# One activation tile and the keys' weight loaded from ScalarE's queue in a linear-attention and MLP kernel on one core

## The chip, the cores and the metric

The kernel runs on 1 core of one Trainium2 chip. The metric is the device time of one execution in microseconds (us), the median over runs. The engines are called as the profile calls them: PE (matmuls), PEld (PE's weight loads), DVE, ACT, POOL, and SP, which here only issues DMAs; "SPq" and "ACTq" mark DMAs issued from SP's and from ACT's instruction stream.

## The reference

```python
def reference(A_x, A_wqkv, A_wo, B_x, B_w1, B_w2):     # x: 1 x 2048 x 512, bf16
    qkv = layernorm(x) @ wqkv                          # 512 -> 3 * 512, 32 heads of 16
    pq, pk = phi(q), phi(k)    # phi(t) = where(t > 0, t + 1, exp(t)) + 1e-6
    kv = einsum("bhsd,bhse->bhde", pk, v)
    z = einsum("bhsd->bhd", pk)
    o = einsum("bhqd,bhde->bhqe", pq, kv) / (einsum("bhqd,bhd->bhq", pq, z) + 1e-6)
    h = x + o @ wo
    return h + maximum(layernorm(h) @ w1, 0) @ w2      # 512 -> 1792 -> 512
```

B_x is not used. Layernorm has no scale and no shift.

## The kernel before

The 2048 rows of x are 16 tiles of 128 rows by 512 columns (128 KB each), tile t lying in `x_nat[:, t, :]`. Four tiles make a chunk, whose transposed layernorm is `lnT[c]`.

Nothing is scheduled by a program at build time: `ORDER`, a string of some 700 words, is read from left to right, and each word calls one small function, which records its instructions on their engines. So the order of words is the order of instructions on every engine, and a word that must wait holds up all later words of the same engine. The digits behind a word's name are its arguments: tile, number of tiles, PSUM bank.

```python
    def op_lx(t, n):
        nc.sync.dma_start(out=x_nat[:, t : t + n, :], in_=rows_of(xf, t, n))
    def op_ax(t, n):
        nc.scalar.dma_start(out=x_nat[:, t : t + n, :], in_=rows_of(xf, t, n))
    def op_ak(k, n):
        nc.scalar.dma_start(out=wk_sb[:, k : k + n, :], in_=wqkv_v[:, k : k + n, D : 2 * D])
    op_lk = lambda k, n: load_d(wk_sb, wqkv_v[:, :, D : 2 * D], k, n)
    ...
    for word in ORDER.split():
        name, *idx = word.split(".")
        ops[name](*map(int, idx))
```

The words at the program's head, with the line that the profile shows for each:

- `lx` (L219) loads tiles of x from SP's queue, `ax` (L222) from ACT's. `lk` (L225, the line of the helper `load_d`) loads the keys' weight, 512 x 512, 512 KB, from SP's queue, `ak` (L228) from ACT's. `lq`, `lv`, `lo`, `l1`, `l2` (all L225) load the other weights from SP's queue.
- `table` (L183) loads ACT's function tables. `const` (L191 to L195) fills constants on DVE, `masks` (L199 to L211) fills masks on POOL. `warm` (L250) runs matmuls on zeros, whose results nobody reads.
- `S.t` (L253) and `A.t` (L254), on DVE: mean and variance of tile t. `R.t` (L259, L260), on ACT: the reciprocal deviation, two instructions. `N.t` (L267), on DVE: the normalised tile.
- `T.t` (L292), on PE: four 128 x 128 transposes of tile t into a bank. `E.t` (L302), on ACT: that bank into `lnT`. From tile 5 on `X.t` (L313) does the same by a transposing DMA from SP's queue.
- `K.t` (L321), on PE: the keys of tile t, four matmuls of 128 x 512 against `wk_sb`. `F`, `U` (L339, L342, ACT), `M`, `D` (L346, L349, DVE) make phi of them. `Q` (L329) are the queries, `G` (L373) the matmuls that gather the keys' statistics.

After them come attention's small products, the MLP's two matmuls (L516 and L525, then L545) and the stores. `T.0`, `T.1`, `T.2` stand ahead of `K.0` on PE, then `K.0`, `K.1`, `T.3` and `K.2`.

A DMA issued from SP or ACT waits where its completion counter is still in use by an earlier DMA; there are eight such counters, handed out in turn.

Of the kernel before, what the change touches and what calls it, by code (L numbers as in the profile page):

```python
# [15 lines left out]


ORDER = """
table const lx.0.1 warm.66.7.64 lx.1.1 masks lx.2.1 lk.0.4 lx.3.1 S.0 lx.4.2 S.1 lx.6.2 lq.0.4 A.0 A.1 S.2 R.0.1
warm.2.7 lx.8.4 R.1.1 N.0 lx.12.4 A.2 N.1 T.0.1 R.2.1 T.1.6 E.0 N.2 E.1 T.2.4 S.3 K.0.2 E.2 A.3 S.4 K.1.4.2.2 R.3.1  # L20
K.1.4.0.2 F.0.1 N.3 A.4 U.0.1 S.5 T.3.5 K.2.6.2.2 E.3 S.7 K.2.6.0.2 F.1.1 K.3.3.0.2 M.0.1 A.5 U.1.1 D.0.1 K.3.3.2.2
M.1.1 R.4.2 Q.0.3.1 S.6 F.3.1 A.7 A.6 N.5 F.2.1 Q.0.1.5 N.4 X.5 R.6.2 D.1.1 T.4.7 U.3.1 M.2.1 Q.0.0.4 M.3.1 S.8 E.4
lo.0.2 U.2.1 S.10 Q.0.2.0 qF.0.0.2 N.6 K.4.2 N.7 X.6 A.10 A.8 qU.0.0.2 S.9 K.5.3 D.3.1 X.7 A.9 D.2.1 R.8.2 G.0 S.15
F.4.2 N.8 G.1 S.13 X.8 U.4.2 S.14 G.3 qU.0.2.2 A.13 S.12 lv.0.2 G.2 M.4.2 A.12 N.9 K.7.3 R.12.2 A.15 D.4.2 X.9
qF.0.2.2 K.6.2 N.12 A.14 S.11 R.14.2 X.12 K.8.0 F.6.2 N.15 N.14 G.4 A.11 N.13 U.6.2 M.6.2 X.13 qM.0.0.2 K.9.1 R.10.2
qD.0.0.2 K.12.2 X.15 D.6.2 U.8.2 za.4.1 G.5 F.8.2 X.14 K.13.3 N.11 N.10 za.6.0 G.6 X.11 U.12.2 G.7 M.8.2 F.12.2 X.10
qM.0.2.2 K.14.0 D.8.2 M.12.2 K.15.1 lv.2.2 za.8.0 l1.0.2 K.11.3 l1.2.2 F.14.2 D.12.2 K.10.2 zf U.14.2 qD.0.2.2 G.9 zhi
F.10.2 M.14.2 G.13 zlo U.10.2 G.8 M.10.2 D.14.2 G.12 D.10.2 z.0.0 z.2.0 z.3.0 z.1.0 G.15 zc zh d4.0.2 G.11 dl4.0 dx4.0
G.14 wb.0 G.10 lo.2.2 Q.1.1.1 gA.2.2 gD.0.2 rb.0.4 Q.1.0.0 ab.0.1 rb.0.6 ab.0.3 kv.1.7 rb.0.2 kv.3.7 ab.0.7 kv.0.7
rb.0.0 kv.2.7 ab.0.5 Q.1.3.3 l2.7.7 kx qF.1.0.2 Q.1.2.2 qU.1.0.2 qM.1.0.2 m.0.4 m.2.6 m.1.5 qF.1.2.2 qD.1.0.2 m.3.7  # L30
Q.2.0.0 mD.0.2 mA.2.2 Q.2.1.1 qU.1.2.2 dm.0.0.2 Q.2.3.7 dm.0.2.2 qF.2.0.2 h.1.6 qM.1.2.2 qD.1.2.2 qU.2.0.2 h.0.2 hD.1
d4.1.4 s.1 Q.3.1.5 a.1 hD.0 nA.1 h.3.0 s.0 dl4.1 x.1 h.2.2 a.0 hD.3 nA.0 Q.2.2.6 s.3 dx4.1 x.0 Q.3.2.0 a.3 hD.2
qF.2.2.2 n.3 wb.1 Q.3.3.1 s.2 qU.2.2.2 x.3 Q.3.0.4 a.2 n.2 qF.3.2.2 qM.2.0.2 x.2 qM.2.2.2 ph.0.3.3.0 qU.3.2.2 qD.2.2.2
ph.0.0.6.0 ph.0.1.7.0 qM.3.2.2 rb.1.7 qU.3.0.2 ph.0.2.2.0 qD.3.2.2 rb.1.3 ph.0.11.1.0 rb.1.5 qD.2.0.2 ph.0.10.0.0
qF.3.0.2 rb.1.6 ph.0.10.0.1 rb.1.1 ph.0.11.1.1 rb.1.0 p.0.5.4 pD.0.10.2 rb.1.4 rb.1.2 ph.0.2.2.1 ph.0.3.3.1 l2.0.7
qM.3.0.2 ph.0.0.6.1 pD.0.2.2 p.0.6.0 ph.0.1.7.1 qD.3.0.2 p.0.4.3 pD.0.0.2 p.0.7.1 pA.0.4.2 dm.1.2.2 d4.2.5.2 dm.1.0.2
p.0.8.2 dl4.2 pD.0.6.2 dl4.3 p.0.9.3 dx4.2 p.0.13.5 dx4.3 pD.0.8.2 wb.2 r.0.4 h.4.7 h.6.0 hD.4 rb.2.3 f.3.1.0.7 rb.2.1
s.4 rb.2.0 a.4 rb.2.6 rb.2.2 p.0.12.4 rb.2.5 rb.2.7 h.7.2 pD.0.12.2 rb.2.4 f.3.1.7.7 wb.3 hD.7 s.7 h.5.4 hD.6
f.2.3.7.7 hD.5 f.1.6.0.7 dm.2.2.2 dm.2.0.2 s.6 rb.3.2 h.8.0 rb.3.7 a.6 s.5 f.1.6.7.7 rb.3.0 hD.8 rb.3.5 rb.3.6 n.4 s.8
rb.3.3 f.2.3.0.7 a.5 rb.3.1 fo.1 rb.3.4 n.5 a.7 x.5 h.9.7 n.7 n.6 fo.2 f.0.0.7.7 x.4 fo.3 dm.3.2.2 h.10.5 x.7 dm.3.0.2  # L40
h.11.6 hD.9 x.6 hD.10 h.13.3 s.10 h.15.2 fd.3.0.2 fd.3.2.2 a.10 a.8 n.10 hD.11 h.14.7 x.10 s.11 f.0.0.0.7 n.8 a.11
hD.15 s.9 p.1.3.5 hD.13 p.1.8.2 hD.14 fo.0 p.1.2.4 s.15 h.12.1 s.14 p.1.9.3 s.13 a.13 p.1.7.7 pD.1.8.2 p.1.6.6 a.9
n.11 r.8.4 n.13 p.1.12.0 n.9 r.4.4 a.14 a.15 x.9 n.14 p.1.11.3 hD.12 pD.1.2.2 p.1.13.1 x.11 p.1.10.2 n.15 pD.1.6.2 x.8
p.1.0.5 pD.1.10.2 p.1.5.4 fd.1.0.2 fd.1.2.2 x.14 p.1.1.6 s.12 pD.1.12.2 f.5.2.7.7 fd.2.0.2 fd.2.2.2 fd.0.0.2 fd.0.2.2
x.15 pD.1.0.2 p.1.4.3 p.2.2.5 pD.1.4.2 f.5.2.0.7 p.2.6.3 fo.5 p.2.7.4 p.2.3.6 pD.2.6.2 p.2.10.1 a.12 n.12 r.12.4
p.2.4.4 pD.2.2.2 x.12 f.7.0.0.7 fd.5.0.2 fd.5.2.2 x.13 f.7.0.7.7 p.2.5.5 fo.7 p.2.11.2 pD.2.4.2 p.2.12.3 pD.2.10.2
p.2.13.4 f.4.6.0.7 pD.2.12.2 p.2.0.5 p.3.2.1 p.3.3.2 f.4.6.7.7 f.6.0.0.7 fo.4 pD.3.2.2 p.3.9.7 p.3.8.6 f.6.0.7.7
pD.3.8.2 p.2.9.1 fo.6 p.2.1.6 fd.6 p.3.1.3 p.3.0.2 p.2.8.0 pD.3.0.2 p.3.11.4 pD.2.0.2 p.3.10.3 pD.2.8.2 p.3.5.2
p.3.6.6 pD.3.10.2 p.3.7.7 p.3.4.1 pD.3.6.2 f.8.3.0.7 pD.3.4.2 p.3.13.7 f.10.5.0.7 p.3.12.6 f.10.5.7.7 pD.3.12.2
f.14.4.0.7 fo.10 fd.10 fd.7 f.15.1.0.14.3.1 f.15.6.0.14.0.2 fo.15.3.1 fd.15.3.1 f.14.4.7.7 fd.4 f.8.3.7.7 f.13.0.0.7  # L50
f.9.7.0.7 f.13.0.7.7 f.11.5.7.7 fo.13 fo.15.0.2 fo.14 fd.15.0.2 f.11.5.0.7 fd.13 fo.8 fd.8 f.9.7.7.7 fo.11 f.12.1.0.7
fo.9 fd.9 fd.11 f.12.1.7.7 fd.14 f.15.2.0.14.2.1 fo.12 fd.12 fo.15.2.1 ad.15.2.1
"""


# [543 lines left out]
```

## Time and profile before

| | before |
|---|---|
| device time, median of 3 runs (lowest to highest) | 168.88 us (168.74 to 168.93) |
| profiled execution: its time | 168.48 us |
| profiled execution: its span | 166.8 us |
| PE busy | 162.6 us, 98% of the span |
| DVE busy | 115.9 us, 69% |
| ACT busy | 49.5 us, 30% |
| 16 DMA engines, queue of SP (q1) | 33.9% of their time |
| 16 DMA engines, queue of ACT (q10) | 0.7% |

The span is what the trace shows, from the first instruction to the last; the profiled execution's own time has 1.7 us more that lies around it. A view of the timeline has start, length, engine, line, operation, output and inputs, shape and count of merged instructions, and in brackets the idle time before them and what ended it. A view by windows has busy time by engine, then the granted PE clock, the share of the DMA engines that was busy, and the rate that they moved. In the chain of waits each row is one piece of the path that ended last. `st` is the output of `S`, `mv` of `A`, `rstd` of `R`, `h_nat` of `N`, `bk` the PSUM banks, `in_A_wqkv_dram` the tensor that holds the weights of queries, keys and values.

### The profile page before, as it was taken

What the parts mean: (1) busy time and instruction counts of PE and PEld (TensorE: products, weight loads), DVE (VectorE), ACT (ScalarE), POOL (GpSimd) and SP (SyncE); (2) the same over time, 40 slices, a digit from 0 to 9 for tenths busy, and PEclk for the clock granted to TensorE, in tenths of its full rate; (3) what the DMA queues carried; (4) which work ended last, traced back from release to release, by engine and by line L of the source; (5) the groups of instructions that cost most, each with busy time, mean ns of one, the idle gap of its engine ahead of it and who ended that gap; (6) DMA issues with size and microseconds to landing.
All of it is one profiled execution on the core that took longest, in us unless ns stands there. A gap on an engine that the chain in (4) does not pass through costs nothing.

```text
span 166.8 us, 2421 instructions
## 1 busy us (share of the span) xinstructions
PE 162.6 (98%) x920; PEld 79.8 (48%) x920; DVE 115.9 (69%) x215; ACT 49.5 (30%) x83; POOL 4.8 (3%) x21
## 2 busy tenths in 40 slices
PE   7999999999999999999999999999999999999993
PEld 7544444454544774444444444444444444464442
DVE  3899999942599979668999899564535484400532
ACT  3899996715777916200000020010000000000000
POOL 7400000000000000000000000000000000000000
PEclk9999999999999999999999999999999999999999
DMA  4975555763752446231352035312000000020122
GB/s 113 346 300 126 125 97 103 276 253 96 170 177 51 111 135 210 72 94 56 111 109 69 0 63 93 100 30 64 0 0 4 31 0 0 7 97 2 44 95 73
DMA packets 26811, 16.28 MB, mean 98 GB/s; under 512 B 16176, under 2 KB 25776, under 8 KB 26800
## 3 DMA queue, kind: packets, MB, share of 16 engines
q1 hardware_dynamic: 26336, 15.84, 33.9%
q10 hardware_dynamic: 464, 0.30, 0.7%
q8 instruction: 7, 0.11, 0.3%
q14 instruction: 4, 0.03, 0.1%
HBM read 9.96 MB, written 2.62 MB: 75 GB/s over the span
## 4 chain that ended last, share of the span: by engine, by line
PE 94%; DVE 2%; DMA 1%; ACT 0%; issue 0%
PE bk L545 29%; PE bk L516 26%; PE bk L321 8%; PE bk L373 8%; PE bk L329 8%; PE bk L501 8%; PE bk L525 3%; DMA x_nat<-in_A_x_dram 1%; DVE st L253 1%; PE bk L445 1%; DVE gT L553 1%; PE bk L397 1%; PE bk L292 1%; PE bk L419 1%; PE bk L431 1%; DVE h_nat L267 0%
## 5 line engine op out<-in xcount | busy, mean ns | idle before, releaser
L545 PE MATMUL bk<-w_sb,at 128*128 128x512 bf16 (+2 forms) x252 | 50.9, 355 | 0.0
L516 PE MATMUL bk<-lnT,w_sb 128*128 128x512 bf16 x200 | 45.6, 379 | 0.0
L536 DVE TENSOR_SCALAR at<-bk 128x1024 bf16<-128x1024 f32 x27 | 32.4, 1220 | 13.6 <-PE bk L516 10.6
L545 PEld LDWEIGHTS <-at 128*128 128x128 bf16 x252 | 23.5, 98 | 25.2 <-DVE at L536 0.3
L516 PEld LDWEIGHTS <-w_sb 128*128 128x128 bf16 x200 | 19.5, 98 | 23.1 <-issue 0.4
L553 DVE SCALAR_TENSOR_TENSOR gT<-bk,rstd,h_nat 128x512 bf16<-128x512 f32 (+2 forms) x18 | 12.1, 688 | 22.6 <-PE bk L545 20.2
L339 ACT ACTIVATE eb<-bk 128x1024 bf16<-128x1024 f32 (+1 forms) x18 | 16.6, 930 | 3.5 <-PE bk L419 1.6
L259 ACT ACTIVATE rstd<-mv,eps 128x2 f32<-128x2 f32 (+2 forms) x14 | 4.1, 294 | 44.4 <-DVE mv L256 41.6
L342 ACT ACTIVATE rb<-bk 128x1024 bf16<-128x1024 f32 (+1 forms) x18 | 16.6, 936 | 0.9 <-PE bk L321 0.9
L501 PE MATMUL bk<-m_sb,pqs 128*128 128x512 bf16 x64 | 15.3, 379 | 0.0
L321 PE MATMUL bk<-wk_sb,lnT 128*128 128x512 bf16 x64 | 15.1, 379 | 0.0
L329 PE MATMUL bk<-lnT,wq_sb 128*128 128x512 bf16 x64 | 15.0, 379 | 0.0
L373 PE MATMUL bk<-at,h_nat 128*128 128x512 bf16 x56 | 13.2, 379 | 0.0
L253 DVE BATCH_NORM_STATS2 st<-x_nat 128x6 f32<-128x512 bf16 x16 | 10.5, 675 | 1.9 <-DMA x_nat<-in_A_x_dram 1.9
L507 DVE TENSOR_TENSOR h_nat<-bk,x_nat 128x512 bf16<-128x512 f32 x16 | 10.7, 679 | 0.9 <-PE bk L501 0.8
L255 DVE BATCH_NORM_STATS2 st<-h_nat 128x6 f32<-128x512 bf16 x16 | 10.8, 687 | 0.2
L501 PEld LDWEIGHTS <-pqs 128*128 128x128 bf16 x64 | 6.3, 98 | 7.6
L373 PEld LDWEIGHTS <-h_nat 128*128 128x128 bf16 x64 | 6.1, 98 | 7.3 <-issue 0.2
L321 PEld LDWEIGHTS <-lnT 128*128 128x128 bf16 x64 | 6.0, 97 | 7.4 <-ACT lnT L302 0.3
L329 PEld LDWEIGHTS <-wq_sb 128*128 128x128 bf16 x64 | 6.1, 98 | 7.1 <-issue 0.2
L346 DVE TENSOR_SCALAR eb<-eb 128x1024 bf16<-128x1024 bf16 (+1 forms) x18 | 6.7, 389 | 0.3 <-ACT eb L339 0.3
L267 DVE TENSOR_SCALAR h_nat<-x_nat,mv,rstd 128x512 bf16<-128x512 bf16 x16 | 6.1, 400 | 0.3 <-ACT rstd L260 0.3
(62 smaller groups left out, 90.8 us busy)
## 6 DMA issues: line engine op xcount, KB each, us to landing
w_sb<-in_B_w_dram SPq DMA_DIRECT2D x4, 896.0 KB, 5.0
rr<-scr SPq DMA_DIRECT2D x28, 64.0 KB, 2.6
out_dram<-gT SPq DMA_DIRECT2D x10, 128.0 KB, 1.9
x_nat<-in_A_x_dram SPq DMA_DIRECT2D x2, 512.0 KB, 7.1
out_dram<-gT SPq DMA_DIRECT2D x11, 64.0 KB, 1.6
x_nat<-in_A_x_dram SPq DMA_DIRECT2D x4, 128.0 KB, 2.2
wk_sb<-in_A_wqkv_dram SPq DMA_DIRECT2D x1, 512.0 KB, 4.2
x_nat<-in_A_x_dram SPq DMA_DIRECT2D x2, 256.0 KB, 4.5
```

Of the source, the lines that this page charges most:

```text
L253: op_S = lambda t: nc.vector.bn_stats(out=st[:, t, :], in_=x_nat[:, t, :])
L255: op_s = lambda t: nc.vector.bn_stats(out=st2[:, t, :], in_=h_nat[:, t, :])
L321: nc.tensor.matmul(bk[:, b, :], lhsT=lnT[c][:, kd, j * P : (j + 1) * P], rhs=wk_sb[:, kd, :], **part(("k", t), KD),)
L329: nc.tensor.matmul(bk[:, b, :], lhsT=wq_sb[:, kd, j * P : (j + 1) * P], rhs=lnT[c][:, kd, :], start=(kd == 0), stop=(kd == KD - 1),)
L339: nc.scalar.activation(out=buf(eb, kind, i, n), in_=bank(at_bank[kind, i], n), func=ACT.Exp)
L342: nc.scalar.activation(out=buf(rb, kind, i, n), in_=bank(at_bank[kind, i], n), func=ACT.Relu)
L373: nc.tensor.matmul(bk[:, KD + kd, :], lhsT=ln_nat[:, t, kd * P : (kd + 1) * P], rhs=pk(t)[:, 0, :], start=(not stated), stop=(len(stated) ...
L501: nc.tensor.matmul(bk[:, b, :], lhsT=pqs[:, (c * KD + jb) % NQ, j * P : (j + 1) * P], rhs=m_sb[:, jb, :], start=(jb == 0), stop=(jb == KD ...
L516: nc.tensor.matmul(bk[:, b, :], lhsT=w1_sb[:, kd, f * P : (f + 1) * P], rhs=lnT[c][:, kd, :], start=(kd == 0), stop=(kd == KD - 1),)
L536: nc.vector.tensor_scalar(out=acts[c % 2][:, f : f + n, :], in0=bank(at_bank["p", c, f], n), scalar1=-1.0, scalar2=0.0, op0=ALU.mult, op1= ...
L545: nc.tensor.matmul(bk[:, b, 0 : w * P], lhsT=acts[c % 2][:, f, j * P : (j + 1) * P], rhs=w2_sb[:, f, k * P : (k + w) * P], **part(("f", t, ...
L553: nc.vector.scalar_tensor_tensor(out=o_t[:, t % NO, cols], in0=bk[:, at_bank["f", t, k], 0 : w * P], scalar=rstd2[:, t : t + 1], in1=h_nat ...
```

## The change

Tile 1 of x (`ax.1.1`) and the keys' weight (`ak.0.4`) are issued from ACT's queue, ahead of the load of ACT's tables. Tiles 0, 2, 3 and the rest of x are issued from SP's queue as before, without tile 1 and the keys' weight between them. The whole table of words is then laid out anew around this; no function and no size changes (some PSUM banks do), and each engine has the instructions that it had, save the two DMAs.

```diff
 ORDER = """
-table const lx.0.1 warm.66.7.64 lx.1.1 masks lx.2.1 lk.0.4 lx.3.1 S.0 lx.4.2 S.1 lx.6.2 lq.0.4 A.0 A.1 S.2 R.0.1
+ax.1.1 const lx.0.1 warm.66.7.64 ak.0.4 lx.2.1 masks table lx.3.1 lx.4.2 lx.6.2 S.0 lq.0.4 lx.8.4 S.1 lx.12.4 A.0 A.1
...
```

On ACT, at the program's head, the two DMAs now stand between the first branch (the barrier that starts all engines) and the table load:

```order
 L594 UNCONDITIONAL_BRANCH
+L222 DMA x_nat<-in_A_x_dram 128x512
+L228 DMA wk_sb<-in_A_wqkv_dram 128x4x512
 L183 ACT_TABLE_LOAD
 L259 ACTIVATE rstd<-mv,eps_77 128x1
```

The table load has moved behind two DMA issues, and R.0, the first user of the tables, still follows it.

On SP, at the program's head, the same two loads are gone (x_nat are tiles of x, wk_sb, wq_sb, wo_sb the weights; the row that stands for three single tiles holds tiles 0, 1, 2 before and tiles 0, 2, 3 now):

```order
 L594 UNCONDITIONAL_BRANCH
 L219 DMA x_nat<-in_A_x_dram 128x512 x3
-L225 DMA wk_sb<-in_A_wqkv_dram 128x4x512
-L219 DMA x_nat<-in_A_x_dram 128x512
 L219 DMA x_nat<-in_A_x_dram 128x1024 x2
 L225 DMA wq_sb<-in_A_wqkv_dram 128x4x512
 L219 DMA x_nat<-in_A_x_dram 128x2048 x2
-L313 DMA_TRANSPOSE lnT_86<-h_nat 128x4x128
 L225 DMA wo_sb<-in_A_wo_dram 128x2x512
-L313 DMA_TRANSPOSE lnT_86<-h_nat 128x4x128 x2
+L313 DMA_TRANSPOSE lnT_86<-h_nat 128x4x128 x3
```

Everything behind tile 2 has moved up by one or two places, and the first half of wo now stands ahead of the first transposing DMA instead of behind it.

On DVE the first fifteen instructions after the constants' five are the same in both kernels, from S.0 to S.5. The first difference lies just behind them, where S.5 and S.7 stood together and now phi's first step M.0 (L346) stands between them (the piece starts with N.3 and A.4):

```order
 L267 TENSOR_SCALAR h_nat<-x_nat,mv,rstd 128x512
 L254 BN_AGGR mv<-st 128x2
-L253 BN_STATS st<-x_nat 128x6 x2
-L346 TENSOR_SCALAR eb<-eb 128x512
-L254 BN_AGGR mv<-st 128x2
-L349 TENSOR_TENSOR pk_lo<-rb,eb 128x512
+L253 BN_STATS st<-x_nat 128x6
 L346 TENSOR_SCALAR eb<-eb 128x512
 L253 BN_STATS st<-x_nat 128x6
+L254 BN_AGGR mv<-st 128x2
```

Up to N.4 and N.5 DVE has the same instructions, in another order.

More of the change, by code (lines that the diff above doesn't have):

```diff
@@ L18 @@
 ORDER = """
-table const lx.0.1 warm.66.7.64 lx.1.1 masks lx.2.1 lk.0.4 lx.3.1 S.0 lx.4.2 S.1 lx.6.2 lq.0.4 A.0 A.1 S.2 R.0.1
[L20 to L52, printed above, removed]
+ax.1.1 const lx.0.1 warm.66.7.64 ak.0.4 lx.2.1 masks table lx.3.1 lx.4.2 lx.6.2 S.0 lq.0.4 lx.8.4 S.1 lx.12.4 A.0 A.1
@@ new lines @@
+warm.2.7 S.2 R.0.1 lo.0.2 R.1.1 N.0 A.2 N.1 T.0.7 R.2.1 T.1.5 E.0 N.2 S.3 E.1 T.2.4 K.0.1 E.2 A.3 S.4 R.3.1 K.1.4.2.2
+F.0.1 N.3 K.1.4.0.2 A.4 U.0.1 S.5 T.3.5 K.2.6.2.2 E.3 M.0.1 K.2.6.0.2 S.7 F.1.1 K.3.0.2.2 A.5 U.1.1 K.3.0.0.2 M.1.1
+S.6 R.4.2 Q.0.3.1 F.2.1 D.0.1 A.7 A.6 F.3.1 Q.0.1.5 N.5 N.4 X.5 R.6.2 D.1.1 T.4.7 U.3.1 S.10 Q.0.0.4 E.4 M.3.1 M.2.1
+U.2.1 N.6 Q.0.2.0 S.8 qF.0.0.2 X.6 K.4.2 N.7 A.10 qU.0.0.2 A.8 S.9 X.7 K.5.3 D.3.1 A.9 D.2.1 R.8.2 G.0 S.15 F.4.2 N.8
+G.1 S.12 X.8 U.4.2 S.13 G.3 qU.0.2.2 S.14 lv.0.2 K.7.3 A.13 M.4.2 A.12 N.9 G.2 R.12.2 A.15 D.4.2 X.9 qF.0.2.2 K.6.2
@@ new lines @@
+N.12 A.14 S.11 R.14.2 X.12 K.8.0 F.6.2 N.15 N.14 G.4 A.11 N.13 R.10.2 M.6.2 X.13 U.6.2 K.9.1 qM.0.0.2 qD.0.0.2 G.5
+X.15 D.6.2 U.8.2 za.4.1 K.12.2 F.8.2 X.14 K.13.3 N.11 N.10 M.8.2 G.6 X.11 U.12.2 qM.0.2.2 D.8.2 G.7 F.12.2 za.6.0 X.10
+K.14.0 M.12.2 K.15.1 lv.2.2 za.8.0 l1.0.2 K.11.3 l1.2.2 F.14.2 D.12.2 K.10.2 zf U.14.2 qD.0.2.2 G.9 zhi F.10.2 G.13
+M.14.2 zlo U.10.2 G.8 M.10.2 D.14.2 G.12 D.10.2 z.0.0 z.2.0 z.1.0 z.3.0 G.15 zc zh d4.0.2 G.11 dl4.0 dx4.0 G.14 wb.0
+G.10 lo.2.2 Q.1.1.1 gA.2.2 gD.0.2 Q.1.0.0 rb.0.4 ab.0.1 rb.0.0 ab.0.3 kv.1.7 rb.0.2 kv.3.7 ab.0.7 kv.0.7 rb.0.6 kv.2.7
@@ new lines @@
+ab.0.5 Q.1.3.3 l2.7.7 kx qF.1.0.2 Q.1.2.2 qU.1.0.2 qM.1.0.2 m.0.4 m.3.7 m.2.6 qF.1.2.2 qD.1.0.2 m.1.5 Q.2.0.0 mD.0.2
+mA.2.2 Q.2.1.1 qU.1.2.2 dm.0.0.2 Q.2.3.7 dm.0.2.2 qF.2.0.2 h.1.6 qM.1.2.2 qU.2.0.2 qD.1.2.2 h.0.2 hD.1 Q.3.1.5 s.1
+d4.1.4 a.1 hD.0 nA.1 h.3.0 s.0 dl4.1 x.1 h.2.2 a.0 hD.3 nA.0 Q.2.2.6 s.3 dx4.1 x.0 Q.3.2.0 qU.2.2.2 a.3 hD.2 Q.3.3.1
+n.3 wb.1 qF.2.2.2 s.2 x.3 Q.3.0.4 a.2 qF.3.2.2 n.2 x.2 ph.0.3.3.0 qU.3.2.2 qM.3.2.2 ph.0.0.6.0 qM.2.2.2 ph.0.1.7.0
+rb.1.7 qU.3.0.2 qD.2.2.2 ph.0.2.2.0 rb.1.5 ph.0.10.0.0 qM.2.0.2 rb.1.6 qF.3.0.2 ph.0.11.1.0 qD.2.0.2 rb.1.1
@@ new lines @@
+ph.0.10.0.1 qD.3.2.2 rb.1.3 ph.0.11.1.1 rb.1.0 ph.0.2.2.1 pD.0.10.2 ph.0.3.3.1 rb.1.4 ph.0.0.6.1 rb.1.2 p.0.5.4
+qM.3.0.2 l2.0.7 pD.0.2.2 ph.0.1.7.1 p.0.6.0 qD.3.0.2 pD.0.0.2 p.0.4.3 p.0.7.1 pA.0.4.2 dm.1.2.2 d4.2.5.2 pD.0.6.2
+p.0.9.3 dl4.2 dl4.3 dm.1.0.2 p.0.13.5 dx4.2 p.0.8.2 dx4.3 wb.2 r.0.4 h.4.7 pD.0.8.2 h.6.0 hD.4 rb.2.3 f.3.1.0.7 rb.2.1
+s.4 rb.2.0 rb.2.6 a.4 rb.2.2 p.0.12.4 rb.2.7 h.7.3 rb.2.5 pD.0.12.2 rb.2.4 f.3.1.7.7 wb.3 hD.6 hD.7 h.5.0 s.7
+f.2.3.7.7 s.6 hD.5 dm.2.2.2 f.1.5.0.7 dm.2.0.2 a.6 rb.3.2 h.8.0 rb.3.7 rb.3.5 f.1.5.7.7 rb.3.6 hD.8 rb.3.1 s.5 rb.3.4
@@ new lines @@
+n.4 f.2.3.0.7 rb.3.3 fo.1 rb.3.0 s.8 x.4 a.5 f.0.0.7.7 a.7 n.5 n.6 n.7 x.5 fo.2 h.10.5 fo.3 x.7 dm.3.0.2 h.9.7
+dm.3.2.2 h.11.6 x.6 hD.9 hD.10 h.13.4 fd.3.0.2 fd.3.2.2 s.10 h.15.2 a.10 a.8 n.10 h.14.7 hD.11 x.10 s.11 f.0.0.0.7 n.8
+hD.15 hD.13 p.1.3.5 a.11 s.9 p.1.8.2 hD.14 p.1.2.4 fo.0 a.9 n.11 p.1.9.3 r.8.4 s.15 r.4.4 s.14 p.1.7.7 s.13 h.12.1
+a.13 pD.1.8.2 p.1.6.6 n.13 p.1.12.0 n.9 a.14 a.15 x.9 hD.12 p.1.11.3 n.14 n.15 pD.1.2.2 p.1.13.1 x.11 p.1.10.2
+pD.1.6.2 fd.2.0.2 fd.2.2.2 p.1.0.5 fd.1.0.2 fd.1.2.2 x.8 pD.1.10.2 p.1.5.4 s.12 x.15 p.1.1.6 pD.1.12.2 f.5.2.7.7
@@ new lines @@
+fd.0.0.2 fd.0.2.2 x.14 pD.1.0.2 p.1.4.3 p.2.2.5 pD.1.4.2 f.5.2.0.7 p.2.6.3 fo.5 p.2.7.4 p.2.10.1 pD.2.6.2 p.2.3.6 a.12
+n.12 r.12.4 p.2.4.4 x.12 pD.2.2.2 f.7.0.0.7 fd.5.0.2 fd.5.2.2 x.13 f.7.0.7.7 p.2.5.5 fo.7 f.4.6.0.7 pD.2.4.2 p.2.11.2
+p.2.12.3 pD.2.10.2 p.3.9.7 p.2.0.5 p.2.13.4 p.3.3.2 pD.2.12.2 p.3.2.1 f.4.6.7.7 f.6.0.0.7 fo.4 pD.3.2.2 p.3.8.6
+f.6.0.7.7 pD.3.8.2 p.2.9.1 fo.6 p.3.1.3 fd.6 p.3.11.4 p.2.1.6 p.3.0.2 p.2.8.0 pD.3.0.2 p.3.7.7 pD.2.0.2 p.3.10.3
+pD.2.8.2 p.3.5.2 p.3.6.6 pD.3.10.2 f.10.5.0.7 pD.3.6.2 p.3.4.1 f.8.3.0.7 pD.3.4.2 p.3.13.7 p.3.12.6 f.10.5.7.7
@@ L53 @@
+pD.3.12.2 f.14.4.0.7 fo.10 fd.10 fd.7 f.15.1.0.14.3.1 f.14.4.7.7 fo.15.3.1 f.15.6.0.14.0.2 fd.15.3.1 fd.4 f.8.3.7.7
+f.13.0.0.7 fo.8 f.9.7.0.7 f.13.0.7.7 f.11.5.7.7 fo.13 fo.15.0.2 fd.13 fo.14 fd.15.0.2 f.11.5.0.7 fd.8 f.9.7.7.7 fo.11
+f.12.1.0.7 fo.9 fd.9 fd.11 f.12.1.7.7 fd.14 f.15.3.0.14.2.1 fo.12 fd.12 fo.15.2.1 ad.15.2.1
 """
```

## The prediction

> **What bounds the kernel now.** The first view is the windows one, cut at the moments at which PE starts and ends its useful stream.
>
> ```profile
> 6.25:6.44 0.19, 0.01 (x1) 0.00 (x1) 0.14 (x1) 0.19 (x1) 0.00 (x0) 1.00 1.25 356
> 6.44:163.10 156.66, 156.66 (x834) 74.84 (x835) 111.20 (x199) 46.47 (x76) 0.00 (x0) 1.00 0.34 95
> 163.10:166.80 3.70, 0.78 (x14) 0.60 (x11) 1.10 (x2) 0.00 (x0) 0.00 (x0) 0.94 0.15 47
> ```
>
> The first busy time is PE's. From 6.44 to 163.10 it is busy for the whole 156.66 us at a granted clock of 1.00, so no engine can save anything there: this stretch gets shorter only with fewer or cheaper matmuls, and the change removes none. Behind it stand 3.70 us of last stores that the change leaves alone. What is left is the head, the 6.44 us until T.2 starts. A busy PE may still hide small stalls, so the second view is PE's timeline around that point.
>
> ```profile
> 6.44 0.40 PE L292 MATMUL bk<-ident,h_nat 128*128 128x128 bf16 x4 [0.19 <-DVE h_nat L267]
> 6.72 2.00 PE L321 MATMUL bk<-wk_sb,lnT 128*128 128x512 bf16 x8
> 8.62 0.40 PE L292 MATMUL bk<-ident,h_nat 128*128 128x128 bf16 x4
> 8.86 1.89 PE L321 MATMUL bk<-wk_sb,lnT 128*128 128x512 bf16 x8
> 10.58 1.89 PE L329 MATMUL bk<-lnT,wq_sb 128*128 128x512 bf16 x8
> ```
>
> Eight matmuls of 512 columns take 10.58 - 8.86 = 1.72 us from start to start, 0.215 each. The eight of K.0 and K.1 start at 6.72 and would be through at 8.44; T.3 starts only at 8.62. So there are 0.18 us of stall in front of T.3, and none that I can see behind it: the end is pinned to the start of T.3. The third view is the chain of waits, which shows what sets T.2.
>
> ```profile
> 0.80 2.05 DMA x_nat<-in_A_x_dram
> 2.87 1.30 DVE st L253 x2
> 4.18 0.14 DVE mv L254 x2
> 4.32 0.65 DVE st L253
> 5.41 0.30 ACT rstd L259
> 5.74 0.21 ACT rstd L260
> 5.97 0.42 DVE h_nat L267
> 6.44 0.40 PE bk L292 x4
> 6.84 1.88 PE bk L321 x8
> ```
>
> It starts with the DMA of tile 0, issued at 0.80 and landed at 2.85. From there DVE runs S.0, S.1, A.0, A.1, S.2 without a pause, then comes the reciprocal deviation of tile 2 on ACT, N.2, T.2. Only the first piece is a wait for memory. Last, what holds T.3 beside that chain, on DVE and on ACT:
>
> ```profile
> 6.64 0.69 DVE L253 BATCH_NORM_STATS2 st<-x_nat 128x6 f32<-128x512 bf16 x1 [0.26 <-DMA x_nat<-in_A_x_dram]
> 8.15 0.41 DVE L267 TENSOR_SCALAR h_nat<-x_nat,mv,rstd 128x512 bf16<-128x512 bf16 x1
> 6.07 1.57 ACT L302 ACTIVATE lnT<-bk 128x512 bf16<-128x512 bf16 x3
> 7.59 0.30 ACT L259 ACTIVATE rstd<-mv,eps 128x1 f32<-128x1 f32 x1
> 7.91 0.20 ACT L260 ACTIVATE rstd<-rstd 128x1 f32<-128x1 f32 x1
> ```
>
> S.3 waits 0.26 us for tile 3, but N.3 at 8.15 follows R.3 (7.91 + 0.20 = 8.11), and R.3 follows E.0 to E.2, which fill ACT from 6.07 on. Those hang on tile 0 as well.
>
> **The change part by part.** The issues at the head and what became of them, from SP's timeline and from the view of DMAs in narrow windows (tiles 0 and 3, then the keys' weight; the last row is tile 2 alone):
>
> ```profile
> 0.80 0.87 SPq L219 DMA_DIRECT2D x_nat<-in_A_x_dram  x2
> 1.72 0.42 SPq L219 DMA_DIRECT2D x_nat<-in_A_x_dram  x1
> 2.18 0.43 SPq L225 DMA_DIRECT2D wk_sb<-in_A_wqkv_dram  x1
> 2.66 0.51 SPq L219 DMA_DIRECT2D x_nat<-in_A_x_dram  x1
> x_nat<-in_A_x_dram SPq DMA_DIRECT2D x1, 128.0 KB, 2.0
> x_nat<-in_A_x_dram SPq DMA_DIRECT2D x1, 128.0 KB, 4.0
> wk_sb<-in_A_wqkv_dram SPq DMA_DIRECT2D x1, 512.0 KB, 4.2
> DMA to landing us min/median/max: 2.2/2.2/2.2
> ```
>
> Tile 0 landed at 2.85, tile 2 at 1.72 + 2.2 = 3.9, the keys' weight at 2.18 + 4.2 = 6.4, tile 3 at 2.66 + 4.0 = 6.66. One issue costs SP some 0.46 us from start to start.
>
> Tile 0: its own issue does not move, it stays SP's first at 0.80, and ACT too was free at 0.80 (below). What changes is that tile 1 sets off beside it instead of 0.46 us behind it. What the DMA engines had to spare in those moments:
>
> ```profile
> 1.80:2.40 0.60, 0.60 (x16) 0.60 (x14) 0.00 (x0) 0.28 (x1) 0.53 (x3) 1.00 0.80 224
> 2.40:3.60 1.20, 1.20 (x27) 1.20 (x25) 0.73 (x2) 0.00 (x0) 0.99 (x5) 1.00 0.82 232
> 3.60:4.40 0.80, 0.80 (x19) 0.80 (x17) 0.80 (x4) 0.11 (x1) 0.68 (x3) 1.00 0.86 116
> 4.40:6.40 2.00, 1.86 (x17) 1.04 (x14) 1.70 (x5) 1.61 (x7) 1.50 (x6) 1.00 1.09 380
> ```
>
> Tile 0's 131 KB at 224 GB/s are 0.585 us, and 80% of the engines' time was taken already. If both tiles are served evenly, tile 0 ends when nearly 262 KB are through. At 224 GB/s that costs 1.17 us, 0.58 more; with the engines filled to 100%, 280 GB/s, it costs 0.94 us, 0.35 more; at the 380 GB/s of the full queue from 4.40 on, 0.69 us, 0.10 more. Nothing is lost where ACT's packets come only behind tile 0's. The bounds are thus 0 and +0.58; a gain is excluded, since tile 0's issue stands where it stood. I take **+0.30**, near the +0.35 of the row of these very moments, a little under it because the last packets of the pair may be tile 1's. One more row says that two queues at once are not free. At 40.6 us four 64 KB transfers were issued from SP and four from ACT at the same time, at 57.2 us eight of the same kind from SP alone (the view by tile, two windows):
>
> ```profile
> L476 ACTq DMA_DIRECT2D rr<-scr x4: 314/402/439, 40.6 to 42.2; - x4
> DMA to landing us min/median/max: 3.0/3.4/3.6
> L476 SPq DMA_DIRECT2D rr<-scr x8: 417/424/532, 57.2 to 60.6; - x8
> DMA to landing us min/median/max: 2.5/2.6/2.6
> ```
>
> The best of the first group took 0.5 us longer than the best of the second, though another load was in flight there too. Of this row the Trainium skill says (DMA: Bandwidth & Descriptors, "Issuing engines are not separate DMA queues") that transfers of both issuers run on the same 16 engines and interleave, and that issuing from two only saves the sequencer's time. By that sentence the change buys 0.46 us of SP's time and nothing else.
>
> Tile 1: it need not come earlier. S.1 started right behind S.0 (2.87 + 0.65 = 3.52), so tile 1 was there by then; an earlier landing buys nothing unless S.0 itself is earlier. S.0's delay passes on in full: DVE has no pause up to S.2, so S.0 to T.2, E.0 to E.2, R.3, N.3 and T.3 all move by the same 0.30.
>
> Tile 3 moves up by one whole 512 KB load on SP and lands about 1 us or more earlier, which takes S.3's 0.26 us away. That is worth at most 8.15 - 8.11 = 0.04 us, because R.3 on ACT comes next and hangs on tile 0. I count it as 0. Tiles 4 to 7 and wq only come earlier.
>
> The keys' weight: issued at about 1.26 instead of 2.18. K.0 needs it at 6.72, now 7.02, and the stall of 0.18 before T.3 can absorb a later K.0. Before, it had SP's queue to itself once its turn came; now it shares with tiles 2 to 7 and wq. I count it as 0; the cover is 7.02 + 0.18 = 7.20, and its loss is rival A.
>
> ACT's two issues push the table load. The rows:
>
> ```profile
> 0.80 1.28 ACT L183 ACT_TABLE_LOAD   x1 [0.80 <-PEq L583]
> 4.29 0.30 ACT L259 ACTIVATE rstd<-mv,eps 128x1 f32<-128x1 f32 x1 [2.21 <-DVE mv L254]
> ```
>
> Two issues of 0.46 put it at 1.72 to 3.00. R.0 waits for DVE until 4.29 and ACT stood idle for 2.21 us before it, so 1.29 us of cover remain. Cost 0.
>
> The order behind the head: up to S.5 DVE's instructions are the same, and up to N.4 and N.5 they are the same set, so N.4 moves only with its chain. wo's first half, now ahead of the first transposing DMA, waits for the counter that the keys' weight holds and is out long before tile 5 is normalised. As PE had no stall after 8.62, the new layout can at best keep that. Count 0, in the bad case some tenths.
>
> Sum: +0.30 on the profiled execution, 168.48 + 0.30 = 168.78 us. The median of the runs stood 0.40 above that execution, and the same lies around it now: 168.88 + 0.30 = 169.18, rounded to **169.2 us**. A difference under 0.2% (0.34 us) can't be told from no change, so the likeliest result lies near the edge of what can be seen.
>
> **The rivals.** A, the keys' weight comes late (ends slower). From the end of tiles 0 and 1, about 2.7, its 524 KB alternate with SP's stream. If each of its 1 KB rows lets one piece of SP's go first, and those of tiles 4 to 7 are two rows long, some 790 KB of SP's pass beside it: 1.31 MB at 380 GB/s are 3.45 us, plus the slow start in the row 3.60:4.40 (0.80 us at 116 GB/s instead of 380 lose 0.56) and about 0.4 to the landing: 2.7 + 3.45 + 0.56 + 0.4 = 7.1. The cover ends at 7.20, from there on each tenth is paid in full; a landing at 7.6 would give +0.7 in all, 169.6. The Trainium skill has the rule (the same page, "Queues, rings and completion order"): an engine goes round the queues that have work, one packet each. No row before 40 us shows two queues, so only the new trace can tell. For A speaks that rule, against it that SP has 0.46 us between issues and cannot fill its queue at once. I give it 0.15.
>
> B, the slow start moves onto the tiles (slower). The weights' tensor is first read from 3.60, 1.42 us after its issue, and until 4.40 the engines were 86% busy for 116 GB/s. Moved to an issue at 1.26 this lies at 2.68 to 3.48, on the last packets of tiles 0 and 1 and on tile 2. It decides when tile 1 lands after S.0's end; the price is up to the lost 0.56 us, beside tile 0's own: 168.88 + 0.3 + 0.4 = 169.6. Against it: both tiles should be through by 2.7. 0.12.
>
> C, the change does not do what it says: ACT's packets come behind tile 0's, and nothing on the path moves. All rows but the first of the chain then stay: 168.9, give or take 0.1. 0.13.
>
> D, faster. The timed runs were 0.40 longer than the profiled one. If that is the late landing of tile 3 or of the keys' weight in those runs, where the trace has 0.26 us of wait, the change takes it away while tile 0 stays unhindered: 168.5. Against it: nothing in the trace says where the 0.40 lies. 0.08.
>
> **How the numbers follow.** The forecast (tile 0 shares the engines, +0.1 to +0.58) has 0.52, of which 0.29 stay under +0.34 and 0.23 lie above. Same: 0.29 + C 0.13 = 0.42. Slower: 0.23 + A 0.15 + B 0.12 = 0.50. Faster: D, 0.08. The range leaves out D and the far end of A and B: from 168.7, under C, to 169.8, where A or B cost 0.6 beside the 0.3.
>
> **What the new profile would show.** Right: both first DMAs issued at 0.80, S.0 starting at about 3.15 instead of 2.87, S.1 behind it without a wait, T.2 at about 6.75, T.3 near 8.9, no wait at S.3, and PE full from there to the end. Wrong: S.0 at 2.87 (C, or faster if T.3 is then earlier than 8.62); a wait at S.1 or S.2 (B); a weight load of L321 that waits for wk_sb after T.2 (A); a stall of PE behind T.3 (the layout).

## The result and the profile after

The changed kernel takes 169.50 us (median of 9 runs, 169.16 to 170.21) against 168.84 us of the kernel before (9 runs, 168.51 to 169.52): a ratio of 1.0044, 95% interval 1.0029 to 1.0060. The change costs 0.66 us between the medians. The profiled execution took 169.97 us with a span of 168.2 us; its own time lies 0.47 above the median, so it shows more loss than the typical run has.

The chain of waits of the changed kernel, its head:

```profile
0.80 2.74 DMA x_nat<-in_A_x_dram
3.56 1.29 DVE st L253 x2
4.99 0.65 DVE st L253
6.41 0.20 ACT rstd L260
6.62 1.53 ACT lnT L302 x3
```

Tile 0 now takes 2.74 us from issue to landing instead of 2.05, and S.0 starts at 3.56 instead of 2.87. All of DVE's head, up to S.2, moves by that 0.69. PE's timeline shows how much of it comes through, and what else was lost:

```profile
7.12 0.40 PE L292 MATMUL bk<-ident,h_nat 128*128 128x128 bf16 x4 [0.30 <-DVE h_nat L267]
7.35 1.89 PE L321 MATMUL bk<-wk_sb,lnT 128*128 128x512 bf16 x8
9.08 0.39 PE L292 MATMUL bk<-ident,h_nat 128*128 128x128 bf16 x4
22.48 1.03 PE L373 MATMUL bk<-at,h_nat 128*128 128x512 bf16 x4
23.56 1.04 PE L321 MATMUL bk<-wk_sb,lnT 128*128 128x512 bf16 x4
104.53 1.03 PE L516 MATMUL bk<-lnT,w_sb 128*128 128x512 bf16 x4
106.16 1.04 PE L516 MATMUL bk<-lnT,w_sb 128*128 128x512 bf16 x4 [0.60 <-DMA lnT<-hn]
```

T.3 starts at 9.08, 0.46 later than in the first profile of before. Four matmuls of 512 columns need 0.86 us from start to start, so PE lost 0.22 us at 23.56 (23.56 - 22.48 - 0.86), waiting for a tile that the transposing DMA brings, and 0.77 us at 106.16, waiting for the last tile of the MLP's third chunk. 0.46 + 0.22 + 0.77 = 1.45, which is the difference of the two spans (1.4). PE was full behind T.3 in the first profile of before; now there are two holes. The SP queue shows where the third loss comes from, before above, after below (L314 is the transposing DMA of the MLP, the word `x`; L560 is a store, the word `fd`):

```profile
96.88 3.81 SPq L314 DMA_TRANSPOSE lnT<-hn  x3
100.73 1.68 SPq L560 DMA_DIRECT2D out_dram<-gT  x2
```

```profile
97.58 2.50 SPq L314 DMA_TRANSPOSE lnT<-hn  x2
100.13 3.47 SPq L560 DMA_DIRECT2D out_dram<-gT  x4
103.64 2.50 SPq L314 DMA_TRANSPOSE lnT<-hn  x2
```

The layout moved four stores (fd.2, fd.1) ahead of the transposing DMA of tile 8, x.8. Before, x.8 was the last of the three transposing DMAs in the first row, issued at 99.43. Now the stores held SP for 3.47 us, x.8 went out at 103.64, and PE needed its tile at 105.39 (104.53 + 0.86).

Back at the head, the windows show what the DMA engines did while tile 0 was late, again before above and after below (the last two columns: busy share of the engines, GB/s):

```profile
1.60:2.00 0.40, 0.40 (x12) 0.40 (x10) 0.00 (x0) 0.40 (x1) 0.33 (x2) 1.00 0.41 97
2.00:2.40 0.40, 0.40 (x12) 0.40 (x10) 0.00 (x0) 0.08 (x1) 0.40 (x2) 1.00 0.79 238
```

```profile
1.60:2.00 0.40, 0.40 (x12) 0.40 (x10) 0.00 (x0) 0.27 (x1) 0.33 (x2) 1.00 0.08 18
2.00:2.40 0.40, 0.40 (x12) 0.40 (x10) 0.00 (x0) 0.40 (x1) 0.40 (x2) 1.00 0.32 64
2.40:2.80 0.40, 0.40 (x12) 0.40 (x10) 0.00 (x0) 0.40 (x1) 0.33 (x2) 1.00 0.95 333
```

In this trace the engines were not overloaded by two tiles: until 2.4 they were 8% and 32% busy. Few bytes moved before 2.4, then the rate was 333 GB/s.

### The profile page after: what moved, and what is told of

Its sections match the earlier page's. It is cut to its first block, busy times and chain, and to the rows that moved or that the text cites. A ratio compares the mean times of both kernels' runs of the same rounds, so it can differ in the third digit from the quotient of the medians.

```text
span 168.2 us, 2418 instructions
## 1 busy us (share of the span) xinstructions
PE 162.9 (97%) x920; PEld 79.6 (47%) x920; DVE 115.6 (69%) x215; ACT 49.4 (29%) x83; POOL 4.7 (3%) x21
## 4 chain that ended last, share of the span: by engine, by line
PE 69%; DVE 15%; DMA 7%; SPq 3%; ACT 3%; issue 1%; DVEq 0%
PE bk L545 25%; PE bk L516 19%; PE bk L329 6%; PE bk L373 6%; PE bk L501 5%; DVE st L253 4%; PE bk L321 4%; PE bk L525 3%; DMA lnT<-hn 3%; DVE st L255 2%; DVE h_nat L507 2%; DMA lnT<-h_nat 2%; SPq L560 2%; DMA x_nat<-in_A_x_dram 2%; DVE gT L553 1%; ACT lnT L302 1%
## 5 line engine op out<-in xcount | busy, mean ns | idle before, releaser
L346 DVE TENSOR_SCALAR eb<-eb 128x1024 bf16<-128x1024 bf16 (+1 forms) x18 | 6.7, 389 | 1.2 <-ACT eb L339 1.1
```

## The experiments

Ratios are to the kernel before, run beside them on the same chip, with 95% intervals. "T.3" and "S.0" are start times in the profile, to be held against the profiles of before. The experiments ran in three sets, in which the median of before was 168.77, 169.08 and 168.91 us; so between sets the ratios are to be compared, not the times.

**The kernel before once more** (no edit). 

> The kernel before once more, for a second profile: its first profile was 0.3 us under the median of its runs. If the head varies from run to run, S.0 is later than 2.87 or S.3 waits longer than 0.26 us for tile 3, and T.3 is at 8.7 to 9.0; if the variation lies behind the head, T.3 is at 8.62 and PE waits for the transposing DMAs near 23 us.

Measured: 168.88 us in one run, close to the median of its set (168.91), where the first profile of before had come from a run of 168.48.

```profile
2.85 1.29 DVE L253 BATCH_NORM_STATS2 st<-x_nat 128x6 f32<-128x512 bf16 x2 [1.60 <-DMA x_nat<-in_A_x_dram]
7.02 0.70 DVE L253 BATCH_NORM_STATS2 st<-x_nat 128x6 f32<-128x512 bf16 x1 [0.65 <-DMA x_nat<-in_A_x_dram]
9.00 0.40 PE L292 MATMUL bk<-ident,h_nat 128*128 128x128 bf16 x4 [0.42 <-DVE h_nat L267]
23.27 1.67 PE L321 MATMUL bk<-wk_sb,lnT 128*128 128x512 bf16 x7
```

Tile 0 is the same, but S.3 waits 0.65 us for tile 3 and T.3 starts at 9.00, not at 8.62. So the head does vary from run to run, by the landing of tile 3 (2.66 + 4.0 = 6.7 there, 2.66 + 4.3 = 7.0 here), and the profile that the forecast was made from was one with an early tile 3. Against this second profile the changed kernel is 0.08 us behind at T.3 (9.08), 0.29 behind in all at 23 us (23.56), and loses 0.77 more at 106: 1.06 of the spans' 1.1.

**The head alone.**

```diff
-table const lx.0.1 warm.66.7.64 lx.1.1 masks lx.2.1 lk.0.4 lx.3.1 S.0 ...   (the order of before)
+ax.1.1 const lx.0.1 warm.66.7.64 ak.0.4 lx.2.1 masks table lx.3.1 S.0 ...
```

> The order of before with the new loads alone: tile 1 and the keys' weight from ACT ahead of the table load, nothing else laid out anew. Theory H (the head is the loss): in the changed kernel's profile T.3 came 0.46 us later than before, the other 1.0 us of its longer span lay in two later stalls. If the head is what the timed runs lose, this kernel is slower by 0.4 to 0.7 us (ratio 1.0024 to 1.0041), with S.0 at about 3.5 and T.3 at about 9.1. Rival L (the new layout is the loss): the later stalls make most of the 0.66 us between the medians; then this one is within 0.3 us of before (ratio under 1.002).

Measured: 168.98 us, ratio 1.0011 (0.9997 to 1.0025).

```profile
9.08 0.39 PE L292 MATMUL bk<-ident,h_nat 128*128 128x128 bf16 x4
23.34 1.67 PE L321 MATMUL bk<-wk_sb,lnT 128*128 128x512 bf16 x7
```

T.3 is at 9.08 as expected, but the time differs by 0.2 us, not by 0.46. Before's own T.3 is not always early: of the five profiles with all loads of the head on SP in the order of before (two of before, the layout alone, and those beside 16 and 128 rows of 8 bytes), two have it near 8.6 and three between 8.93 and 9.00. The interval holds zero: the head alone is not shown to lose anything. Theory H asked for 1.0024 or more, where the interval all but ends; rival L's band holds the measured ratio.

**The layout alone** (the order of the changed kernel, its head put back).

```diff
-ax.1.1 const lx.0.1 warm.66.7.64 ak.0.4 lx.2.1 masks table lx.3.1 lx.4.2 ...   (the order of after)
+table const lx.0.1 warm.66.7.64 lx.1.1 masks lx.2.1 lk.0.4 lx.3.1 lx.4.2 ...
```

> The changed kernel's order with all loads issued from SP as before, so the layout alone. Theory H: the ratio is 0.999 to 1.0015, S.0 at 2.87 and T.3 at 8.6. Rival L: slower by 0.4 us or more (ratio over 1.0024), with PE stalls behind 8.6, above all before the MLP's third chunk near 105 us, where four stores now stand ahead of the last transposing DMA on SP.

Measured: 169.16 us, ratio 1.0029 (1.0011 to 1.0047). From its PE timeline and its SP queue:

```profile
103.82 1.03 PE L516 MATMUL bk<-lnT,w_sb 128*128 128x512 bf16 x4
105.08 1.04 PE L516 MATMUL bk<-lnT,w_sb 128*128 128x512 bf16 x4 [0.23 <-DMA lnT<-hn]
```

```profile
99.42 3.09 SPq L560 DMA_DIRECT2D out_dram<-gT  x4
102.56 2.50 SPq L314 DMA_TRANSPOSE lnT<-hn  x2
```

By the ratio the layout loses 0.5 us without any of the moved loads. In its profile T.3 is at 8.59, as in the first one of before; the hole in front of x.8's tile has 0.40 us (105.08 - 103.82 - 0.86), and the span is 0.3 longer than before's. Rival L holds. Head and layout add up to 1.0040, close to the whole 1.0044.

**The transposing DMA first.** One word of the changed kernel's order moves, and only SP's sequence changes:

```diff
-pD.1.6.2 fd.2.0.2 fd.2.2.2 p.1.0.5 fd.1.0.2 fd.1.2.2 x.8 pD.1.10.2
+pD.1.6.2 x.8 fd.2.0.2 fd.2.2.2 p.1.0.5 fd.1.0.2 fd.1.2.2 pD.1.10.2
```

> The changed kernel with one edit: on SP the last transposing DMA of the MLP's third chunk (x.8) stands ahead of the four stores again, as in before. Theory L (the layout's loss is this place: PE waited 0.77 us there in the changed kernel's profile and 0.39 in the layout alone): no wait of PE for lnT near 105 us, and the time falls by 0.3 to 0.6 us against the changed kernel's 1.0044, to a ratio of 1.001 to 1.0025. Rival (the wait is paid anyway, in another place): the ratio stays at 1.0035 to 1.005.

Measured: 169.17 us beside 169.08, ratio 1.0010 (0.9993 to 1.0026).

```profile
104.49 1.89 PE L516 MATMUL bk<-lnT,w_sb 128*128 128x512 bf16 x8
106.22 1.67 PE L545 MATMUL bk<-w_sb,at 128*128 128x512 bf16 x7
```

The hole is gone (eight matmuls in 1.73 us), and the ratio falls to that of the head alone; its interval ends at 1.0026, and that of the changed kernel begins at 1.0029. The four stores ahead of x.8 are the larger part of the loss.

**Tile 1 alone from ACT.**

```diff
-table const lx.0.1 warm.66.7.64 lx.1.1 masks lx.2.1 lk.0.4 lx.3.1 S.0 ...   (the order of before)
+ax.1.1 table const lx.0.1 warm.66.7.64 masks lx.2.1 lk.0.4 lx.3.1 S.0 ...
```

> The order of before with tile 1 alone issued from ACT ahead of the table load; the keys' weight stays on SP and is issued one place earlier. Theory B (bytes: tile 0 waits because tile 1's packets share the 16 engines with its own): tile 0 lands 0.3 to 0.6 us later than 2.85, and T.3 comes 0.2 to 0.5 later. Theory W (the weight's 512 KB behind tile 1 make it as late as 3.54): tile 0 lands within 0.15 us of 2.85. Theory G (two issuers starting at once slow each other's start, whatever the bytes): 3.4 to 3.6 as in the changed kernel. Ratio 1.0 under W, 1.001 to 1.003 under B and G.

Measured: 169.18 us, ratio 1.0026 (1.0012 to 1.0040). S.0 starts at 3.57, so tile 0 is late by 0.7 without the keys' weight on ACT's queue: theory W falls. The delay is over theory B's 0.3 to 0.6 and inside theory G's band. The DMA engines from 1.60 to 2.40, then S.3 and T.3:

```profile
1.60:2.00 0.40, 0.40 (x12) 0.40 (x10) 0.00 (x0) 0.40 (x1) 0.34 (x1) 1.00 0.59 51
2.00:2.40 0.40, 0.40 (x12) 0.40 (x10) 0.00 (x0) 0.40 (x1) 0.40 (x2) 1.00 0.63 128
```

```profile
7.89 0.69 DVE L253 BATCH_NORM_STATS2 st<-x_nat 128x6 f32<-128x512 bf16 x1 [0.83 <-DMA x_nat<-in_A_x_dram]
9.87 0.40 PE L292 MATMUL bk<-ident,h_nat 128*128 128x128 bf16 x4 [0.39 <-DVE h_nat L267]
```

Here the engines were 59% and 63% busy and still moved only 51 and 128 GB/s. So the idle engines of the changed kernel's trace are not what the late tiles have in common; the few bytes until 2.4 are. Tile 3 still comes behind the weight on SP's queue, lands at 2.19 + 5.7 = 7.9, and T.3 is at 9.87 (in a run of 169.75, 0.57 over the median, so this profile shows more loss than most runs have). With the weight on ACT, too, tile 3 lands early enough for T.3 to stand at 9.08.

**What may set off beside tile 0.** Four kernels put another DMA of ACT's at 0.80, all else as in before: 16 rows of 8 bytes (`tx.16`), 128 rows of 8 bytes (`tx.128`), tile 15 of x (`ax.15.1`, loaded again later), and 128 rows of 1 KB of wo, by a new word `ao`.

```diff
-table const lx.0.1 ...     (the order of before)
+tx.16 table const lx.0.1 ...      tx.128 / ax.15.1 / ao.0.1 in its place in the others
```

> The order of before with one tiny DMA (16 rows of 8 bytes of x, into a tile that nobody reads) issued from ACT ahead of its table load, at the same moment as tile 0; all real loads on SP as before. Theory B (bytes): 128 bytes cost nothing, tile 0 lands at 2.85 and the ratio is within 0.001 of 1. Theory G (starting two issuers at once): tile 0's first packets still come late, it lands at 3.1 to 3.5, ratio 1.001 to 1.003.

> The order of before with a DMA of 128 rows of 8 bytes of x (1 KB in all, into a tile that nobody reads) issued from ACT at the same moment as tile 0: as many rows as tile 1 has, with 1/128 of its bytes. Theory B (bytes share the engines): nothing moves, tile 0 lands at 2.85 to 3.0 as beside the 16 rows. Theory R (the two issuers' rows are prepared by something that they share, so the count of rows matters): tile 0 lands at 3.3 to 3.6 as beside tile 1, with the engines little busy between 1.8 and 2.4.

> The order of before, with tile 15 (128 rows of 1 KB of x, loaded a second time later) issued from ACT at the same moment as tile 0, and tile 1 on SP as before. Beside tile 1 from ACT, tile 0 landed 0.65 to 0.7 us later in four kernels; beside 128 rows of 8 bytes or beside the keys' weight it did not. Theory B (bytes of a second transfer that has its data at once): tile 0 lands at 3.4 to 3.6 again. Rival N (only a neighbour in memory does it): tile 0 lands at 2.85 to 3.05.

> The same with 128 rows of 1 KB of the output weight (loaded a second time later) in place of tile 15: as many rows and bytes, another tensor. Theory B: tile 0 lands at 3.4 to 3.6. Rival N, or a rival by which only a second reader of the same tensor does it: 2.85 to 3.05.

Measured: 16 rows, ratio 1.0004 (0.9990 to 1.0017), S.0 at 2.96. The other three in single runs: 169.13, 171.44 and 170.12 us. DMA issues in the first moments, KB and us to landing, in this order: 128 rows of 8 bytes, tile 15, wo.

```profile
x_nat<-in_A_x_dram SPq DMA_DIRECT2D x1, 128.0 KB, 2.2
first_x<-in_A_x_dram ACTq DMA_DIRECT2D x1, 1.0 KB, 2.4
```

```profile
x_nat<-in_A_x_dram ACTq DMA_DIRECT2D x1, 128.0 KB, 3.3
x_nat<-in_A_x_dram SPq DMA_DIRECT2D x1, 128.0 KB, 3.1
```

```profile
wo_sb<-in_A_wo_dram ACTq DMA_DIRECT2D x1, 128.0 KB, 2.9
x_nat<-in_A_x_dram SPq DMA_DIRECT2D x1, 128.0 KB, 2.7
```

As many rows with 8 bytes each cost tile 0 at most 0.2, against 0.65 to 1.1 beside 128 rows of 1 KB, from the same tensor or another. Even the 0.2 is not shown to be their doing: with all loads on SP (tile 3 ahead of the weight, below) S.0 stood at 3.00. Theory R and rival N fall, and theory G's 3.1 to 3.5 was not reached beside the 16 rows. Bytes are needed (theory B), though not as B had it: the engines did not run at their full rate while tile 0 was late. Nor does every load with bytes do it: beside the keys' weight, issued at 0.82 in the last experiment, S.0 started at 3.08. Why that one did not is open.

**Staggered.** The kernel with the transposing DMA first, and the tiny DMA ahead of tile 1 on ACT, so that tile 1 starts at 1.24.

```diff
-ax.1.1 const lx.0.1
+tx.16 ax.1.1 const lx.0.1
```

> The changed kernel with the transposing DMA ahead of the four stores, and a DMA of 16 rows of 8 bytes ahead of tile 1 on ACT, so that tile 1 sets off at 1.2 instead of 0.80. If it is the common start that costs tile 0 its 0.65 us, tile 0 lands at 2.85 to 3.05, T.3 comes at 8.5 to 8.8, and the time is 0.1 to 0.4 us under that of the kernel with the transposing DMA first (ratio 0.998 to 1.0005 to before). If sharing at any moment costs it, tile 0 lands at 3.2 or later and the ratio is 1.0005 to 1.002.

Measured: 169.34 us, ratio 1.0039 (1.0014 to 1.0063).

```profile
2.90 0.69 DVE L253 BATCH_NORM_STATS2 st<-x_nat 128x6 f32<-128x512 bf16 x1 [1.66 <-DMA x_nat<-in_A_x_dram]
4.09 0.69 DVE L253 BATCH_NORM_STATS2 st<-x_nat 128x6 f32<-128x512 bf16 x1 [0.50 <-DMA x_nat<-in_A_x_dram]
```

Tile 0 is back at 2.90, but tile 1, now starting together with SP's tile 2, lands at 1.24 + 2.8 = 4.04, and S.1 waits for it. T.3 is again at 9.09. The delay has moved from one tile to the next. The expected gain did not come. Two of the twelve runs, 170.81 and 171.14 us, raise the ratio; the other ten have a mean of 169.31 against 168.97 of before, 1.0020, which is inside the interval of the kernel that this one was made from. Why these two runs are long is open.

**Tile 3 ahead of the weight, all on SP.**

```diff
-lk.0.4 lx.3.1 S.0
+lx.3.1 lk.0.4 S.0
```

> The order of before with tile 3 issued ahead of the keys' weight on SP, all on SP. Theory E (an earlier tile 3 is worth something in most runs, since T.3 hangs on it when it lands after 6.6): tile 3 lands before 5, S.3 follows N.2 without a wait, the time falls by 0 to 0.4 us (ratio 0.998 to 1.0) if the weight, 0.46 us later, still lands by 6.9. Rival (the weight takes tile 3's place as the last to come): K.0 waits for it, ratio 1.001 to 1.003.

Measured: 169.12 us beside 169.08, ratio 0.9999 (0.9978 to 1.0021).

```profile
8.59 0.40 PE L292 MATMUL bk<-ident,h_nat 128*128 128x128 bf16 x4
23.23 1.90 PE L321 MATMUL bk<-wk_sb,lnT 128*128 128x512 bf16 x8 [0.21 <-DMA lnT<-h_nat]
```

S.3 no longer waits and T.3 starts at 8.59, 0.41 earlier than in the second profile of before. At 23 us PE waits for the transposing DMA and is where the second profile of before was, 23.23 against 23.27. The gain at T.3 is given back there. The first profile of before, with T.3 at 8.62, had no such wait (these matmuls started at 22.89), so the wait is not there in every run either.

**The weight behind the table load.**

```diff
-table const lx.0.1 warm.66.7.64 lx.1.1 masks lx.2.1 lk.0.4 lx.3.1 S.0 ...   (the order of before)
+table const lx.0.1 warm.66.7.64 lx.1.1 masks lx.2.1 ak.0.4 lx.3.1 S.0 ...
```

> The order of before with the keys' weight alone issued from ACT, behind the table load (at about 2.1), so that no two issuers start at once at 0.80. Tile 0 lands at 2.85 as before under every theory. Theory E: tile 3, now issued at 2.18 instead of 2.66, lands before 6, and the time falls by 0 to 0.3 us (ratio 0.998 to 1.0). Rival: the weight's rows hold up tile 3 on the other queue as they did on their own, tile 3 lands at 6 to 7, ratio 0.9995 to 1.001.

Measured: 171.92 us (median of 6), ratio 1.0154 (1.0119 to 1.0189), outside what any theory gave. From the timelines of ACT, ACT's queue and DVE, then a row of the windows view, then PE's timeline:

```profile
0.79 1.28 ACT L183 ACT_TABLE_LOAD   x1 [0.79 <-PEq L583]
0.82 0.47 ACTq L228 DMA_DIRECT2D wk_sb<-in_A_wqkv_dram  x1
5.82 0.69 DVE L253 BATCH_NORM_STATS2 st<-x_nat 128x6 f32<-128x512 bf16 x1 [2.04 <-DMA x_nat<-in_A_x_dram]
8.00:10.00 2.00, 1.93 (x13) 1.07 (x12) 1.68 (x5) 1.91 (x6) 0.00 (x0) 0.50 1.07 394
9.18 2.65 PE L321 MATMUL bk<-wk_sb,lnT 128*128 128x512 bf16 x8
11.67 0.39 PE L292 MATMUL bk<-ident,h_nat 128*128 128x128 bf16 x4
```

The DMA did not wait for the table load: it was issued at 0.82, while the tables were loading. So the weight did set off beside tile 0, which the experiment was meant to avoid. Tile 0 still landed for S.0 at 3.08, but tile 1, issued on SP at 1.25, was there only for S.1 at 5.82, after the 512 KB of the other queue (0.82 + 4.6 = 5.4). A part of the loss is a lower clock, not a wait: PE stood idle for 2.83 us before T.0, and from 8 to 10 us the granted clock was 0.50. K.0 and K.1 took 2.49 us there (11.67 - 9.18) instead of 1.72, so 0.77 of the 2.67 us that T.3 lies behind the second profile of before are the clock's. Five of the six runs have a mean clock of 0.988 to 0.990 and take 171.52 to 172.38 us; the one at 1.00 takes 170.43. The kernel with tile 15 beside tile 0 had the same in its single run (0.56 and 0.59 from 8 to 12 us), so its 171.44 us do not price tile 0's delay.

No kernel of these beat the one before; the best is the even one with tile 3 first.

## Why the forecast came out as it did

The direction was right, and 169.2 us lies 0.3 under the measured 169.50, inside the range of 168.7 to 169.8, but that is partly luck: the sum charged the head, and most of the loss lies behind it. By its steps:

- **Tile 0 shares the engines, +0.30, bounds 0 and +0.58.** Right in place, wrong in size: it landed 0.69 later, above the upper bound. That bound counted bytes at the rates of one queue; until 2.4 us both tiles together moved at far less than these rates (18 and 64 GB/s in the changed kernel, 51 and 128 with tile 1 alone; before had 97 and 238), which no row of before could show.
- **Tile 3's earlier landing, counted as 0, "worth at most 0.04".** Mis-sized. For the profile that it was read from it holds, but the 0.26 us of wait came from one run; in the second profile of before the wait is 0.65 and T.3 stands at 9.00, 0.38 later. In such a run most of tile 0's delay is hidden behind tile 3: 9.08 after against 9.00 before. Nor did tile 3 land "about 1 us or more earlier": it landed at 1.72 + 4.3 = 6.0 in the changed kernel and at 1.72 + 5.2 = 6.9 with the head alone, against 6.7 and 7.0 before. The two wrong terms nearly cancelled, and the head alone costs 0.2 us with an interval that holds zero.
- **The order behind the head, counted as 0.** This is the step that failed. By the ratios the layout alone costs 0.5 us of 0.7 (0.0029 and 0.0044 of 168.8), most of it by four stores ahead of one transposing DMA on SP, a place that the order shows and the forecast did not look at: it compared the orders up to N.4 and N.5 only. Its "in the bad case some tenths" has the size; its own test "a stall of PE behind T.3 (the layout)" names what was found.
- **"The end is pinned to the start of T.3."** Only in part. With T.3 0.41 us earlier than in the second profile of before, PE waited at 23 us instead and nothing was gained; and the changed kernel's holes at 23 and 106 us lie behind T.3.
- **The keys' weight, rival A.** It did not come late: 1.23 + 4.5 = 5.7 after, 1.25 + 5.4 = 6.7 with the head alone, inside the cover of 7.20.
- **The table load, cost 0.** Right: it ran from 1.73 to 3.01, R.0 waited for DVE until 4.97.
- **Rival B** (a slow start of the weight on the tiles) did not happen: tile 0 was as late without the weight beside it. **Rival C** was wrong. **Rival D** had the place right as far as one more profile can say: a run 0.40 us longer than the first had T.3 0.38 later, by tile 3's landing. But the change moved tile 3 at tile 0's expense.

## What to carry to other kernels

A table of orders that is laid out anew must be read to its end, queue by queue: look for a transfer that somebody waits for and that has new, slower neighbours ahead of it. One profile of a kernel whose runs spread by some tenths of a per cent is one draw; where a wait for memory sets a term, take a second profile before the term is sized. And a second issuing engine was no second lane here: tile 0, for which the path waited, landed 0.65 us or more later beside 128 KB that set off with it on ACT's queue.
